# Attention and a gated MLP on one core: which loads release which weight parts in the first tile

## The chip, the cores and the metric

The kernel runs on 1 core of one Trainium2 chip. The metric is the time of one execution on the device in microseconds (us); the time of a kernel is the median of its runs.

## The reference

Sliding-window causal attention (window 64) over 8 batches of 8 heads, 576 tokens and 64 values per head, and then a feed-forward layer with a gate on its result:

```python
B, H, S, D = q.shape                                   # 8, 8, 576, 64
scores = np.matmul(q, k.transpose(0, 1, 3, 2)) / np.sqrt(D)
rel = pos[:, None] - pos[None, :]
scores = np.where((rel >= 0) & (rel < 64), scores, -1e9)
attn = np.exp(scores - scores.max(-1)); attn /= attn.sum(-1) + 1e-09
x = np.matmul(attn, v).transpose(0, 2, 1, 3).reshape(B * S, H * D)   # 4608 x 512
h = x @ w_in                                           # w_in: 512 x 2048
g = h * np.clip(h + 3.0, 0.0, 6.0) / 6.0
out = g @ w_out                                        # w_out: 2048 x 512
```

Inputs and output are f32; the matmuls of the kernel are in bf16.

## The kernel before

**Tiles.** The layer is computed in nine tiles T of 512 tokens, the attention in eight batches of 576. `s1(T)` (L523) makes the 16 column blocks `fc` of the gated hidden layer: four matmuls with `win16` per block, one activation on ScalarE and one gate operation on VectorE. Block `fc` uses columns 128 fc to 128 fc + 127 of w_in. `s2(T, order)` (L560) multiplies by `wout16`; a piece of it is four matmuls for one of four token groups and one quarter of w_out's rows. For tile 0 the order is BY_PART (L582): all four token groups with quarter 0, then all with quarter 1, and so on. Attention pieces of the next batches are put by hand between the pieces of `s1` and `s2`: T_ and TT (transposes of Q and K on TensorE, with their copies out of PSUM), S_ (scores), N_ (values and normalisation), X_ (transpose of the result into `xT`), R_ and RR (the transposes of the remainder rows, tokens 512 to 575 of each head, which are loaded apart).

**Order.** The schedule is manual: every engine executes its instructions in the order of the program text, and so do the DMA queues of SyncE (SP) and GpSimd (POOL). A queue whose next load waits holds all that stand behind it. `after(x, y, why)` (L68) makes instruction x wait until y is done; for a load, until it has landed.

**Weights.** They are loaded on POOL's queue, cast from f32 to bf16 on the way, in four parts each: w_in by 512 columns (`load_w_in`, L225), w_out by 512 rows (`load_w_out`, L231). A part has 1 MB in memory and 512 KB in SBUF. Part i of w_in serves blocks 4 i to 4 i + 3. POOL also casts all Q, K and V to bf16, so in its order casts (which wait for loads) and weight loads alternate: w_in part 0 at L645, part 1 at L648, parts 2 and 3 at L650, w_out part 0 at L721, parts 1 to 3 at L723.

**Q, K, V.** They are loaded on SP's queue. Batch 0 comes first (L140, L82). For batch 1 `load_qk_for_pe(1, 4)` (L100) returns in this order: `ins[0]`, `ins[1]`: Q and K of heads 0 to 3 (512 KB each, L107); `ins[2]`, `ins[3]`: remainder rows of Q and K (128 KB each, L113); `ins[4]`, `ins[5]`: Q and K of heads 4 to 7. Then follow `insr[:2]`, the remainder rows of Q and K of batch 0 (L151), and `insv`: the remainder of V of batch 0, and V of batch 1 (L94, L82). Behind them stand the loads of batches 2 and up (L94), and the DMA transposes and output writes.

**The releases.** `ins[0]` and `ins[1]` wait for w_in part 1 (L704); `ins[2:]` and `insr[:2]` for w_out part 0 (L724); `insv` for w_out part 2 (L726). Since SP goes in order, each wait holds all later loads too.

**The stretch of the change (L697 to L765).** `m = s1(0, ...)` makes tile 0. Its first groups of matmuls and the blocks 0 to 3 are 6 steps of the generator, of which 2 are taken at once (L698, L700); `run(m, 12)` (L731) goes to the end of block 11. Then `TT(bt, 0)` transposes Q and K of the first pair of heads of batch 1, which needs the POOL casts of heads 0 to 3; two blocks follow, `TT(bt, 1)`, and the last two blocks. Then `s2(0)` starts: scores of two pairs, four pieces with w_out part 0, `RR(bt)` (L760) with the remainder rows of batch 1 (cast at L728), and the pieces with part 1.

Of the kernel before, what the change touches and what calls it, by code (L numbers as in the profile page):

```python
# [24 lines left out]
def kernel(  # L25
# [14 lines left out]
    NG = H // 2  # L40
# [27 lines left out]
    def after(ins, dep, why):  # L68

        tc.add_manual_dep(  # L70
            ins.ins, dep.ins.name,
            mybir.DependencyInfo(mybir.DependencyClass.Sync, mybir.DependencyReason.DATA),
            reason=why,
        )
# [25 lines left out]
    def load_qk_for_pe(b, heads):  # L100
        qst = stage.tile([P, H, R * D], F32, name="qst", tag="qst")
        kst = stage.tile([P, H, R * D], F32, name="kst", tag="kst")
        rst = stage.tile([P, H, D], F32, name="rst", tag="rst")
        ins = []
        for h0 in range(0, H, heads):
            for dst, src in ((qst, q), (kst, k)):
                ins.append(nc.sync.dma_start(  # L107
                    out=dst[:, h0 : h0 + heads, :],
                    in_=src[b, h0 : h0 + heads, 0:SM, :].rearrange("h (p j) d -> p h (j d)", j=R),
                ))  # L110
            if h0 == 0:
                for i, src in enumerate((q, k)):
                    ins.append(nc.sync.dma_start(  # L113
                        out=rst[i * SR : (i + 1) * SR, :, :],
                        in_=src[b, :, SM:S, :].rearrange("h s d -> s h d"),
                    ))
        return (qst, kst, rst), ins

    def load_v_by_head(b):
        vst = stage.tile([P, KB, H, D], F32, name="vst", tag="vst")  # L120
        ins = load_blocks(vst, v, b, (KB - 1,), SR) + load_v(b, vst, 0, H)
        return vst, ins
# [23 lines left out]
    def load_rest_of_first():  # L146
        rst = stage.tile([P, H, D], F32, name="rst0", tag="rst0")
        rvst = stage.tile([P, H, D], F32, name="rvst", tag="rvst")
        ins = []
        for dst, p0, src in ((rst, 0, q), (rst, SR, k), (rvst, SR, v)):  # L150
            ins.append(nc.sync.dma_start(  # L151
                out=dst[p0 : p0 + SR, :, :], in_=src[0, :, SM:S, :].rearrange("h s d -> s h d"),
            ))
        return rst, rvst, ins
# [70 lines left out]
    def load_w_in(f0, f1, g0, g1):  # L225
        return nc.gpsimd.dma_start(
            out=win16[:, g0:g1, f0:f1],
            in_=moe_w_in[g0 * P : g1 * P, f0:f1].rearrange("(g p) f -> p g f", p=P),
        )

    def load_w_out(c0, c1):  # L231
        return nc.gpsimd.dma_start(
            out=wout16[:, c0:c1, :],
            in_=moe_w_out[c0 * P : c1 * P, :].rearrange("(c p) j -> p c j", p=P),
        )


    vcopy, pcopy, acopy = nc.vector.tensor_copy, nc.gpsimd.tensor_copy, nc.scalar.copy
# [284 lines left out]
    def s1(T, first=()):  # L523
        t0 = T * TB
        gT = gpool.tile([P, NFC, TB], BF16, name="gT")
        gTs[T] = gT

        def mms(fc, hT, gs):
            for g in gs:
                nc.tensor.matmul(  # L530
                    hT, lhsT=win16[:, g, fc * P : (fc + 1) * P],
                    rhs=xT[:, g, t0 : t0 + TB], start=(g == 0), stop=(g == NG - 1),
                )

        def gate(out, hT, shape):
            t1 = (t1pool, t2pool)[len(shape) - 2].tile(shape, BF16, name=f"t{len(shape) - 1}")
            nc.scalar.activation(out=t1[:], in_=hT, func=RELU, bias=half[:], scale=1.0 / 6.0)  # L537
            nc.vector.scalar_tensor_tensor(  # L538
                out=out, in0=t1[:], scalar=1.0, in1=hT, op0=MIN, op1=MULT,
            )  # L540

        if first:
            sts = [ps_st.tile([P, 2, 512], F32, name=f"st{u}") for u in range(2)]
            for gs in first:
                for fc in range(4):
                    mms(fc, sts[fc // 2][:, fc % 2, :], gs)
                yield
            for u in range(2):
                for fc in (2 * u, 2 * u + 1):
                    mms(fc, sts[u][:, fc % 2, :], (NG - 1,))  # L550
                gate(gT[:, 2 * u : 2 * u + 2, :], sts[u][:], [P, 2, TB])
                yield
                yield
        for fc in range(4 if first else 0, NFC):
            hT = s1_bank(fc, T)
            mms(fc, hT, range(NG))
            gate(gT[:, fc, :], hT, [P, TB])
            yield

    def s2(T, order):  # L560

        gT, accs = gTs[T], {}
        for ts, f0, f1 in order:
            if f0 == 0:
                accs[ts] = h_bank()[:] if T == 0 and ts > 1 else next(oa)
            for fc in range(f0, f1):
                nc.tensor.matmul(  # L567
                    accs[ts], lhsT=gT[:, fc, ts * P : (ts + 1) * P], rhs=wout16[:, fc, :],
                    start=(fc == 0), stop=(fc == NFC - 1),
                )  # L570
            if f1 == NFC:
                osb = osbp.tile([P, DM], F32, name="osb")
                acopy(out=osb[:], in_=accs[ts])  # L573
                u0 = T * TB + ts * P
                if T:
                    nc.sync.dma_start(out=out[u0 : u0 + P, :], in_=osb[:])
                else:
                    held.append((u0, osb))
            yield
# [4 lines left out]
    def run(gen, n=10 ** 6):  # L584
        for _ in range(n):
            if next(gen, "end") == "end":
                break
# [32 lines left out]
    def TT(bt, g, banks=None):  # L620
        T_(bt, g, banks)
        do(bt, "q", g)
        do(bt, "k", g)
# [12 lines left out]
    def cast_pairs(bt, st, h0, heads):  # L636
        bt.cast_qk(st, 0, h0, heads, pcopy)
        bt.cast_qk(st, 1, h0, heads, pcopy)


    bt, st = Batch(0), stage0
# [3 lines left out]
    w_in = [load_w_in(0, 512, 0, NG)]  # L645
# [1 line left out]
    bt.cast_v(vst0, 4, 6, pcopy)  # L647
    w_in.append(load_w_in(512, 1024, 0, NG))  # L648
    bt.cast_v(vst0, 6, 8, pcopy)
    w_in += [load_w_in(512 * i, 512 * (i + 1), 0, NG) for i in (2, 3)]  # L650
    pcopy(out=bt.V[0:SR, KB - 1, :, 0:D], in_=bt.V[SR:P, KB - 2, :, 0:D])

    def S0_(g, u):
# [43 lines left out]
    m = s1(0, ((0, 1), (2,)))  # L697
# [5 lines left out]
    st1, ins = load_qk_for_pe(1, 4)  # L703
# [3 lines left out]
    rst0, rvst0, insr = load_rest_of_first()  # L707
    vst1, insv = load_v_by_head(1)
    insv = insr[2:] + insv
# [5 lines left out]
    for h in range(2):  # L715
        nc.vector.tensor_copy(
            out=mask[:, (KB - 1) * (h + 1) - 1, P:QW], in_=mask1[:, WINDOW : 2 * WINDOW],
        )
    bt, st = Batch(1), st1
    bt.cast_qk(st, 0, 0, 4, pcopy)  # L720
    w_out = [load_w_out(0, 4)]  # L721
    bt.cast_qk(st, 1, 0, 4, pcopy)
    w_out += [load_w_out(4 * i, 4 * i + 4) for i in (1, 2, 3)]  # L723
    for x in ins[2:] + insr[:2]:  # L724
        after(x, w_out[0], "the weights go first")
    for x in insv:  # L726
        after(x, w_out[2], "the weights go first")
    bt.cast_rest(st, pcopy)  # L728
    cast_pairs(bt, st, 4, 4)
    bt0.cast_rest((None, None, rst0), pcopy)  # L730
    run(m, 12)  # L731
    TT(bt, 0, oa_tr)
    run(m, 2)
    TT(bt, 1, oa_tr)
# [21 lines left out]
    m = s2(0, BY_PART)  # L756
# [124 lines left out]
```

## Time and profile before

| | us |
|---|---|
| median of 7 runs | 326.93 |
| lowest, highest | 323.26, 328.76 |
| profiled execution, whole | 328.82 |
| its span, first to last instruction | 327.1 |
| TensorE (PE) busy | 307.1 |
| VectorE (DVE), ScalarE (ACT), GpSimd (POOL) busy | 178.9, 177.7, 90.0 |

| load on POOL's queue | issued at | landed after |
|---|---|---|
| w_in part 0 | 11.0 | 6.5 |
| w_in part 1 | 13.4 | 7.8 |
| w_in part 2 | 14.7 | 9.1 |
| w_in part 3 | 15.5 | 12.4 |
| w_out part 0 | 29.8 | 5.4 |
| w_out part 1 | 31.5 | 8.4 |
| w_out part 2 | 32.3 | 10.9 |
| w_out part 3 | 33.0 | 13.5 |

| load on SP's queue | issued at | landed after |
|---|---|---|
| Q, K of heads 0 to 3, batch 1 | 21.3, 21.8 | 7.3, 8.3 |
| remainder rows of Q, K, batch 1 | 35.2, 36.0 | 8.5, 10.7 |
| Q, K of heads 4 to 7, batch 1 | 36.7, 37.5 | 11.5, 13.0 |
| remainder rows of Q, K, batch 0 | 40.0, 43.1 | 11.1, 8.7 |
| V of batch 1, 8 loads | 48.1 to 53.7 | 3.6 to 3.7 |

All times within the trace count from the start of the span. PE is the matmul side of TensorE, PEld its weight loads, POOLq and SPq the two queues that issue DMAs. A name such as `st` or `h` is a PSUM tile, `win` and `wout` are the weights in SBUF, `qst`, `kst`, `vst` and `rst` the loaded f32 inputs, `qn`, `kn` and `rn` their casts. In "out<-in" the first is written. The granted clock is TensorE's, as a share of full speed.

### The profile page before, as it was taken

The page shows a single profiled execution, that of the slowest core. Times are in us where ns is not written, and L with a number is a line of the kernel's source. Part 1 is how long each engine was busy: PE and PEld are TensorE (multiplying, and loading weights), DVE is VectorE, ACT ScalarE, POOL GpSimd, SP SyncE. Part 2 cuts the span into 40 slices and gives each one's busy share as a digit, 9 for nine tenths or more (in the row PEclk, how much of TensorE's full clock was granted, in tenths as well). Part 3 has the DMA queues.
Part 4 walks back from the last instruction along what each step waited for, and adds up shares of the span by engine and source line. Part 5 has one row for each costly group of instructions (what it writes and reads, how often), then busy time and mean ns, then how long its engine had stood idle before and what let it go on. Part 6 is the DMA issues. An engine that isn't in the chain of part 4 may idle for free.

```text
span 327.1 us, 5618 instructions
## 1 busy us (share of the span) xinstructions
PE 307.1 (94%) x2162; PEld 149.7 (46%) x2162; DVE 178.9 (55%) x334; ACT 177.7 (54%) x264; POOL 90.0 (28%) x128
## 2 busy tenths in 40 slices
PE   7996929979999999999999999999999999999995
PEld 3543414554455445544444454445444544444442
DVE  4666404556674585657835773687178618505800
ACT  3765504537773685379416951794279327516711
POOL 6804117464047143405600353044300000000000
PEclk9999878979999999999999999999999999999999
DMA  7994999899899999889749998999950260020011
GB/s 252 206 195 140 178 255 195 190 214 235 177 196 211 243 213 219 210 173 206 144 125 257 199 212 164 248 198 203 193 132 2 72 118 22 0 93 37 0 66 64
DMA packets 151515, 52.80 MB, mean 161 GB/s; under 512 B 138944, under 2 KB 147136, under 8 KB 151488
## 3 DMA queue, kind: packets, MB, share of 16 engines
q1 hardware_dynamic: 146672, 46.94, 71.2%
q0 software_dynamic: 4544, 5.24, 9.2%
q8 instruction: 17, 0.28, 0.4%
q10 hardware_dynamic: 272, 0.26, 0.2%
q14 instruction: 10, 0.08, 0.1%
HBM read 36.70 MB, written 9.44 MB: 141 GB/s over the span
## 4 chain that ended last, share of the span: by engine, by line
PE 76%; DMA 12%; DVE 6%; ACT 2%; SPq 1%; issue 1%; POOL 1%; POOLq 0%
PE acc L567 17%; PE o L567 16%; PE h L530 15%; PE st L530 6%; PE o L530 6%; PE acc L530 6%; PE st L353 4%; DMA qst<-in_q_dram 4%; DMA rst<-in_k_dram 3%; DMA win<-in_moe_w_in_dram 2%; PE h L383 2%; DMA wout<-in_moe_w_out_dram 2%; DVE gT L538 2%; DVE pT L371 2%; DVE opg L405 2%; PE h L388 1%
## 5 line engine op out<-in xcount | busy, mean ns | idle before, releaser
L530 PEld LDWEIGHTS <-win 128*128 128x128 bf16 x576 | 55.9, 99 | 67.9 <-issue 4.2
L567 PEld LDWEIGHTS <-gT 128*128 128x128 bf16 x576 | 52.9, 98 | 57.9 <-issue 1.6
L567 PE MATMUL o<-wout,gT 128*128 128x512 bf16 x272 | 66.8, 383 | 0.0
L567 PE MATMUL acc<-wout,gT 128*128 128x512 bf16 x272 | 64.8, 383 | 0.0
L530 PE MATMUL h<-xT,win 128*128 128x512 bf16 x264 | 63.1, 379 | 0.0
L361 ACT ACTIVATE pT<-st 128x768 bf16<-128x768 f32 x64 | 48.7, 808 | 15.5 <-PE st L353 15.4
L538 DVE SCALAR_TENSOR_TENSOR gT<-t,st 128x512 bf16<-128x512 bf16 (+1 forms) x26 | 20.7, 809 | 62.2 <-ACT t L537 62.2
L537 ACT ACTIVATE t<-h,half 128x512 bf16<-128x512 f32 x66 | 44.7, 691 | 8.4 <-PE h L530 7.9
L538 DVE SCALAR_TENSOR_TENSOR gT<-t,h 128x512 bf16<-128x512 bf16 x66 | 44.6, 685 | 7.9 <-ACT t L537 7.9
L371 DVE TENSOR_TENSOR pT<-pT,mask 128x1536 bf16<-128x1536 bf16 x28 | 33.2, 1184 | 22.6 <-ACT pT L361 22.5
L257 POOL CAST qn<-qst 128x512 bf16<-128x512 f32 x24 | 15.6, 689 | 78.5 <-DMA qst<-in_q_dram 78.5
L530 PE MATMUL st<-xT,win 128*128 128x512 bf16 x128 | 32.6, 399 | 0.4 <-DVE gT L538 0.3
L573 ACT COPY osb<-acc 128x512 f32<-128x512 f32 x17 | 10.0, 586 | 41.8 <-PE acc L567 41.8
L573 ACT COPY osb<-o 128x512 f32<-128x512 f32 x17 | 10.0, 588 | 30.2 <-PE o L567 30.2
L405 DVE TENSOR_TENSOR opg<-h,rec 128x320 bf16<-128x320 f32 x48 | 23.6, 491 | 1.7
L537 ACT ACTIVATE t<-st,half 128x512 bf16<-128x512 f32 (+1 forms) x26 | 20.1, 785 | 7.8 <-PE st L530 7.8
L530 PE MATMUL o<-xT,win 128*128 128x512 bf16 x92 | 23.6, 379 | 0.3 <-DVE gT L538 0.3
L530 PE MATMUL acc<-xT,win 128*128 128x512 bf16 x92 | 23.6, 379 | 0.0
L383 PEld LDWEIGHTS <-pT 128*128 128x128 bf16 x256 | 17.7, 98 | 8.8 <-DVE opg L405 1.9
L257 POOL CAST kn<-kst 128x512 bf16<-128x512 f32 x24 | 16.1, 708 | 17.6 <-DMA kst<-in_k_dram 17.6
L247 POOL CAST V<-vst 128x512 bf16<-128x512 f32 (+1 forms) x14 | 16.4, 1170 | 14.3 <-DMA vst<-in_v_dram 12.4
L353 PE MATMUL st<-QT,KT 64*128 64x192 bf16 (+2 forms) x312 | 17.6, 232 | 1.0 <-ACT KT L321 0.5
(100 smaller groups left out, 281.5 us busy)
## 6 DMA issues: line engine op xcount, KB each, us to landing
out_dram<-osb SPq DMA_DIRECT2D x32, 256.0 KB, 2.3
qst<-in_q_dram SPq DMA_DIRECT2D x28, 256.0 KB, 4.6
kst<-in_k_dram SPq DMA_DIRECT2D x27, 256.0 KB, 5.3
vst<-in_v_dram SPq DMA_DIRECT2D x24, 256.0 KB, 5.4
vst<-in_v_dram SPq DMA_DIRECT2D x23, 128.0 KB, 3.7
win<-in_moe_w_in_dram POOLq DMA_DIRECT2D x4, 512.0 KB, 8.5
wout<-in_moe_w_out_dram POOLq DMA_DIRECT2D x4, 512.0 KB, 9.7
qst<-in_q_dram SPq DMA_DIRECT2D x2, 512.0 KB, 9.4
```

Of the source, the lines that this page charges most:

```text
L247: copy(out=self.V[:, 0 : KB - 1, h0:h1, 0:D], in_=vst[:, 0 : KB - 1, h0:h1, :])
L257: pcopy(out=n[:, g, 0 : KB - 1, :, :].rearrange("p k h d -> p k (h d)"), in_=s[:, 0 : KB - 1, 2 * g : 2 * g + 2, :].rearrange("p k h d -> ...
L353: nc.tensor.matmul(st[:, h, o0 : o0 + n], lhsT=bt.KT[h * D : (h + 1) * D, g, k0 : k0 + P], rhs=bt.QT[h * D : (h + 1) * D, g, q0 : q0 + n], ...
L361: nc.scalar.activation(out=pT[:, :, 2 * u : 2 * u + 2, 0:QW], in_=st[:, :, 0:w].rearrange("p h (k w) -> p h k w", k=2), func=EXP, scale=scale,
L371: nc.vector.tensor_tensor(out=pT[:, :, :, 0:QW], in0=pT[:, :, :, 0:QW], in1=mask[:].rearrange("p (h k) w -> p h k w", h=2), op=MULT,)
L383: nc.tensor.matmul(ob, lhsT=pT[:, h, qb, 0:P], rhs=V[:, qb, 2 * g + h, :], start=True, stop=(qb == 0),)
L405: nc.vector.tensor_tensor(out=opgs[bt.b, g][:, 0:nb, h, :], in0=ov[:, :, 0:D], in1=rec[:, 0:nb].unsqueeze(2).to_broadcast([P, nb, D]), op= ...
L530: nc.tensor.matmul(hT, lhsT=win16[:, g, fc * P : (fc + 1) * P], rhs=xT[:, g, t0 : t0 + TB], start=(g == 0), stop=(g == NG - 1),)
L537: nc.scalar.activation(out=t1[:], in_=hT, func=RELU, bias=half[:], scale=1.0 / 6.0)
L538: nc.vector.scalar_tensor_tensor(out=out, in0=t1[:], scalar=1.0, in1=hT, op0=MIN, op1=MULT,)
L567: nc.tensor.matmul(accs[ts], lhsT=gT[:, fc, ts * P : (ts + 1) * P], rhs=wout16[:, fc, :], start=(fc == 0), stop=(fc == NFC - 1),)
L573: acopy(out=osb[:], in_=accs[ts])
```

## The change

The last part of w_in and the last three of w_out are released by loads of Q and K, and these by other weight parts than before:

- w_in part 3 is issued on POOL later: after the loads of batch 1 are set up, ahead of the first cast of batch 1, and it waits for `ins[0]` (Q of heads 0 to 3).
- `ins[2:]` wait for w_in part 3 instead of w_out part 0.
- The cast of the remainder rows (`cast_rest`) moves ahead of w_out parts 1 and 2 on POOL; these wait for `ins[4]` (Q of heads 4 to 7).
- w_out part 3 moves behind the casts of Q and K of heads 4 to 7.
- `insr[:2]` wait, as `insv` do, for w_out part 2.
- `run(m, 11)` instead of 12: block 11 follows `TT(bt, 0)`, block 13 follows `TT(bt, 1)`.

```diff
     bt.cast_v(vst0, 6, 8, pcopy)
-    w_in += [load_w_in(512 * i, 512 * (i + 1), 0, NG) for i in (2, 3)]
+    w_in.append(load_w_in(1024, 1536, 0, NG))
     pcopy(out=bt.V[0:SR, KB - 1, :, 0:D], in_=bt.V[SR:P, KB - 2, :, 0:D])
...
     bt, st = Batch(1), st1
+    w_in.append(load_w_in(1536, 2048, 0, NG))
+    after(w_in[3], ins[0], "the first heads go first")
     bt.cast_qk(st, 0, 0, 4, pcopy)
     w_out = [load_w_out(0, 4)]
     bt.cast_qk(st, 1, 0, 4, pcopy)
-    w_out += [load_w_out(4 * i, 4 * i + 4) for i in (1, 2, 3)]
-    for x in ins[2:] + insr[:2]:
-        after(x, w_out[0], "the weights go first")
-    for x in insv:
+    bt.cast_rest(st, pcopy)
+    for x in ins[2:]:
+        after(x, w_in[3], "the weights go first")
+    w_out += [load_w_out(4 * i, 4 * i + 4) for i in (1, 2)]
+    after(w_out[1], ins[4], "the last heads go first")
+    for x in insr[:2] + insv:
         after(x, w_out[2], "the weights go first")
-    bt.cast_rest(st, pcopy)
     cast_pairs(bt, st, 4, 4)
+    w_out.append(load_w_out(12, 16))
     bt0.cast_rest((None, None, rst0), pcopy)
-    run(m, 12)
+    run(m, 11)
     TT(bt, 0, oa_tr)
     run(m, 2)
     TT(bt, 1, oa_tr)
```

## The prediction

> **What bounds the kernel now.** I read, in this order, the page's slices, the waits of TensorE, the chain of work in the first 72 us, the busy table by microsecond, and the landing times of the loads. The waits (engine and line that waited, releaser: us in total, times, longest):
>
> ```profile
> PE st L298 <- POOL rn L293: 6.0, 1, 6.0
> PE st L463 <- DVE opg L405: 2.0, 1, 2.0
> PE o L316 <- POOL qn L286: 1.5, 1, 1.5
> PE acc L316 <- POOL kn L286: 1.3, 1, 1.3
> ```
>
> TensorE is busy for 307.1 of 327.1 us; all its waits of over 1.3 us lie before 71 us. The stage table (us, then busy us of PE, PEld, DVE, ACT, POOL, the granted clock, DMA share, GB/s) shows the one hole, and a later stage without any:
>
> ```profile
> 41.50:47.50 6.00, 0.00 (x0) 0.00 (x0) 0.00 (x0) 0.00 (x0) 0.62 (x1) 0.80 1.16 271
> 171.00:203.00 32.00, 32.00 (x235) 15.70 (x233) 19.78 (x36) 18.50 (x28) 10.71 (x13) 1.00 1.04 207
> ```
>
> So what moves the restart at 47.5 us moves the end, unless a later load catches up. The chain (start, us, what) tells what the hole waits for:
>
> ```profile
> 13.42 7.85 DMA win<-in_moe_w_in_dram
> 21.32 7.35 DMA qst<-in_q_dram
> 28.82 0.98 POOL qn L286
> 29.80 5.38 DMA wout<-in_moe_w_out_dram
> 35.98 10.74 DMA rst<-in_k_dram
> 46.84 0.62 POOL rn L293
> 47.51 0.61 PE st L298 x4
> ```
>
> It is DMA all along: Q of heads 0 to 3, then w_out part 0, then the remainder rows of K, which take 10.7 us for 128 KB beside the three other parts of w_out. Between the links the DMA stands nearly still (last two columns):
>
> ```profile
> 26.00:27.00 1.00, 1.00 (x7) 0.45 (x5) 1.00 (x3) 0.82 (x2) 0.00 (x0) 1.00 0.99 327
> 28.00:29.00 1.00, 0.40 (x2) 0.00 (x0) 0.81 (x2) 0.82 (x2) 0.18 (x1) 1.00 0.10 36
> 30.00:31.00 1.00, 0.31 (x4) 0.14 (x4) 0.65 (x1) 0.00 (x0) 1.00 (x2) 1.00 0.00 0
> 31.00:32.00 1.00, 0.35 (x4) 0.35 (x5) 0.04 (x1) 0.00 (x0) 1.00 (x2) 0.71 0.27 39
> 46.00:47.00 1.00, 0.00 (x0) 0.00 (x0) 0.00 (x0) 0.00 (x0) 0.16 (x1) 0.50 1.09 351
> ```
>
> About 3.5 us of DMA time (27.5 to 31) are unused.
>
> **Landing times of before,** issue plus time to landing from the views of the tiles: w_in parts 17.5, 21.3, 23.8, 27.9; Q and K of heads 0 to 3 28.7 and 30.1; w_out parts 35.2, 39.9, 43.2, 46.5; remainder rows of batch 1 43.7 and 46.7; Q and K of heads 4 to 7 48.2 and 50.5; remainder Q of batch 0 51.1.
>
> **The change, part by part.** No matmul, cast or load is added or removed; loads change places and releases.
>
> *w_in part 3 behind Q of heads 0 to 3.* Q was issued at 21.3 and landed 0.8 us after w_in part 3. Now w_in part 2 (23.8) is the last weight ahead: 24.6 by that row. From the other side: Q's 512 KB run for 1.5 us at the 350 GB/s of the table, after a 3.7 us landing of a 256 KB K load: 26.5. I take 25.3, nearer the row of the same load. On POOL the wait stands ahead of the Q cast, which needs the same Q, so only the issue (0.75) is put before it: issue 25.3, Q cast 26.1 to 27.1, w_out part 0 issued 27.1 to 27.9, K cast to 28.9.
>
> *w_in part 3 lands* 5.4 us after its issue (w_out part 0, alone on the wires, took 5.4; w_in part 0 beside V took 6.5): 30.7. w_out part 0 follows in the same queue; parts follow each other by 3.3 us (39.9, 43.2, 46.5): 34.0, or 32.5 if alone.
>
> *SP queue.* The remainder loads of batch 1 wait for w_in part 3 instead of w_out part 0: 30.7 instead of 35.2, and behind them at the spacings of before Q of heads 4 to 7 at 32.2 and its K at 33.0. One weight part is in flight beside them, not three. Q lands after w_out part 0 (34.0), the 256 KB of remainder rows (1.3 us at 200 GB/s) and its own 1.5 us: 36.8. Bounds: 3.7 us after issue (35.9), and the 11.5 us it took before (43.7). I lean to the low one, since that row had three parts of w_out beside it.
>
> *w_out parts 1 and 2* now wait on POOL for that Q. Behind the waiting instruction stand the casts of Q and K of heads 4 to 7 and w_out part 3. Issue 36.8, landing 5.4 later: 42.2 (8.4, the row of part 1, at worst: 45.2). Part 2 lands at 45.5. The casts run at 38.3 to 40.4; part 3 is issued at 40.4 and lands at 48.8.
>
> *TensorE.* Column block 11 of tile 0 moves behind the first transposes (0.86 us of matmuls beside a cast wait); block 12 waits for w_in part 3 (30.7). From block 12 to the hole TensorE took 32.05 to 41.5, 9.4 us, so the first four quarter sums are done by 40.1, or 1.4 us sooner if the eight matmuls of 3.27 us run at full clock. The remainder rows are cast by then. The 6.0 us wait is gone; late next is w_out part 1: the first matmuls that need it ran at 47.91 and now run at 42.2. **Gain 5.7 us.** Everything before it is covered by the wait for w_out part 1; were that gone, the gain would end at 40.1, 7.8 us.
>
> *Clock.* The matmuls after the hole ran at 0.50 until about 49.9: 1.91 us for four instead of 1.04. The new idle time is about 2 to 3 us, not 6. Between no half clock (1.1 us won) and a stretch like 32 to 34 (1.4 us lost), I count no difference. The Trainium skill (TensorE: Matmul & The Clock Gate, Part 1) has the half clock come after at least one idle window of about 3.4 us; by it alone the new wait would often stay at full clock and the gain be 6.8.
>
> *The queue that is moved past.* Remainder rows of batch 0, V of batch 1 and with them all later loads wait on SP for w_out part 2: 45.5 instead of 40.0. They were held before by K of heads 4 to 7 (50.5). The remainder Q of batch 0 lands 3.7 us (nearest V row) to 8.5 us (remainder row beside weights) after issue, 49.2 to 54.0, against 51.1: d = -1.9 to +2.9; with one part of w_out left to pass I take 0. Slack in before: first V pair cast by 55.9, used at 62.60, 6.7 us; K transposes of batch 2 landed 79.7, used 88.3; of batch 3 111.1, used 118.5, 7.4 us; of batch 4 136.6, used 149.2. So the gain is the smaller of 5.7 and 6.7 - d: it holds up to d = 1.0, and 3.8 is left at d = 2.9.
>
> *A rule that speaks otherwise.* The rows price a 512 KB weight load alone at 5.4 us. The Trainium skill (DMA: Bandwidth & Descriptors, Anatomy of one DMA) gives about 2.0 us plus bytes over 436 GB/s, an estimate of 3.2 us here. By it the two loads in the chain would land 4.4 us sooner, and no wait for w_out part 1 would be left. It also means that each hand-over costs about 2 us of latency, which speaks against releasing loads by landings.
>
> **Sum.** The profiled execution took 328.82 us, 327.1 of it span and 1.7 around it. 328.82 - 5.7 = 323.1. It stands 1.9 above the median of 326.93. As TensorE is full after 71 us, I place the spread of 323.26 to 328.76 in the start (an estimate); a median run may have 1.9 us less of this stall, a gain of 3.8 to 5.7. The middle, 4.75, off the median: 322.2 us.
>
> **Rivals.**
> 1. *No new wait:* w_out part 1 lands by 40.1. For it: Q and part 1 each at their lower bound give 35.9 + 5.4 = 41.3, so it needs still earlier links; against it: w_out part 0 is ahead. Gain 7 to 7.8: about 319.5.
> 2. *Given back:* V of batch 1 and what follows come late because their release moved from 40.0 to 45.5. For it: SP issues in order and slices up to 230 us show the DMA nearly full. Against it: Q of heads 4 to 7 is done 11 us sooner (48.2 to 36.8). At d = +5.5 the gain is 6.7 - 5.5 = 1.2: 325.7. The same time comes if Q of heads 0 to 3 lands no earlier than 28.7: the chain of 16.9 us (25.3 to 42.2) ends at 45.6, gain 2.3, 324.6.
> 3. *Slower:* Q of heads 4 to 7 is held on the wires by w_out part 0 and keeps its 11.5 us. It lands at 43.7, w_out part 1 at 49.1 to 52.1, TensorE restarts 1.2 to 4.2 after 47.91: 328.1 to 331.1. It decides from a Q landing later than 42.5. For it: 128 KB took 10.7 us beside weights; against it: one part, done by 34.
> 4. *The release does nothing:* excluded for w_in part 3, which had no wait and was issued at 15.5.
>
> **How the numbers follow.** A measurement of this kernel can tell about 1%, 3.3 us. Forecast 0.58 (0.06 of it within 1%, from the small end of its gain); rival 1 0.08, faster; rival 2 0.20 (0.18 within, 0.02 faster); rival 3 0.14 (0.10 slower, 0.04 within). Faster 0.62, same 0.28, slower 0.10. The range: low 318.5 (rival 1 and a microsecond of clock), high 327.5, past rival 2; the upper part of rival 3 is left out. The forecast's own: 320 to 324 (gain 3.8 less, or 5.7 plus, a microsecond of clock).
>
> **What would show it.** Right: the 6.0 us wait for rn is gone; Q of heads 0 to 3 lands near 25, w_in part 3 near 31, Q of heads 4 to 7 near 37; TensorE waits about 2 to 3 us for w_out at about 42; T = 1 starts (71.0 before) near 65.3; no load wait above 1 us after that. Wrong: w_out part 1 after 45, a wait for V or for the transposes of batch 2 or 3, or Q of heads 0 to 3 still at 28.

## The result, and the profile after

The changed kernel takes 323.86 us (median of 26 runs, 320.5 to 325.82), the kernel before 326.56 us (61 runs): ratio 0.9921, 95% interval 0.9900 to 0.9942. It is faster by 0.8%, 2.7 us, where 1.4% was forecast; 323.86 us lies just inside the 320 to 324 us that the prediction gave as the forecast's own. The profiled execution took 324.55 us, 322.8 of it span, against 328.82 and 327.1.

The waits of TensorE after the change (engine and line, releaser: us in total, times, longest):

```profile
PE o L567 <- DMA wout<-in_moe_w_out_dram: 5.8, 1, 5.8
PE st L463 <- DVE opg L405: 2.0, 1, 2.0
PE o L168 <- DVE xT L163: 1.3, 1, 1.3
```

The 6.0 us wait for the remainder rows and the two waits for casts (1.5 and 1.3) are gone. One of 5.8 us for w_out part 1 has taken their place. The chain (start, us, what) shows how it comes about:

```profile
24.51 5.27 DMA win<-in_moe_w_in_dram
29.80 0.71 SPq L113
31.23 6.81 DMA qst<-in_q_dram
38.33 5.50 DMA wout<-in_moe_w_out_dram
43.87 1.86 PE o L567 x4
```

Q of heads 0 to 3 lands at 24.2, more than four microseconds sooner than before, and w_in part 3 is issued on it at 24.5. From there each load of the chain is released by the landing of the last: w_in part 3 lands at 29.8, Q of heads 4 to 7 at 38.0, w_out part 1 at 43.8. In the stage table (us, busy us of PE, PEld, DVE, ACT, POOL, granted clock, DMA share, GB/s) two of the three hand-overs are holes in the DMA, and after the wait TensorE runs at half clock:

```profile
25.00:26.00 1.00, 1.00 (x7) 0.42 (x5) 1.00 (x3) 0.81 (x2) 0.96 (x2) 1.00 0.17 25
36.00:38.00 2.00, 2.00 (x13) 1.04 (x12) 0.00 (x0) 0.03 (x1) 0.61 (x1) 1.00 0.65 205
38.00:40.00 2.00, 0.12 (x3) 0.01 (x1) 0.29 (x1) 0.37 (x1) 1.67 (x3) 1.00 0.03 11
40.00:42.00 2.00, 0.00 (x0) 0.00 (x0) 0.00 (x0) 0.00 (x0) 2.00 (x3) 1.00 0.98 162
44.00:46.00 2.00, 2.00 (x10) 0.58 (x8) 0.00 (x0) 0.00 (x0) 0.00 (x0) 0.50 1.21 196
48.00:50.00 2.00, 2.00 (x11) 0.79 (x12) 0.70 (x2) 0.81 (x1) 0.00 (x0) 0.52 1.13 219
```

Between the landing of Q and the first bytes of w_out part 1 the DMA moves 11 GB/s for two microseconds; after the landing of Q of heads 0 to 3 it moves 25 GB/s for one. At the hand-over of 29.8 there is no hole, since w_out part 0 is under way.

### The profile page after: what moved, and what is told of

It is laid out like the page before. It is cut to its first block, busy times and chain, and to the rows that moved or that the text cites. A ratio compares the mean times of both kernels' runs of the same rounds, so it can differ in the third digit from the quotient of the medians.

```text
span 322.8 us, 5617 instructions
## 1 busy us (share of the span) xinstructions
PE 306.5 (95%) x2162; PEld 149.3 (46%) x2162; DVE 176.3 (55%) x334; ACT 177.7 (55%) x264; POOL 89.2 (28%) x128
## 4 chain that ended last, share of the span: by engine, by line
PE 79%; DMA 8%; DVE 4%; issue 3%; ACT 2%; SPq 2%; POOL 1%; POOLq 0%
PE acc L567 18%; PE o L567 17%; PE h L530 15%; PE st L530 6%; PE o L530 6%; PE acc L530 6%; PE st L353 4%; DMA qst<-in_q_dram 4%; PE h L383 2%; DMA wout<-in_moe_w_out_dram 2%; DVE gT L538 2%; DMA win<-in_moe_w_in_dram 2%; PE h L567 1%; PE h L388 1%; DVE opg L405 1%
## 5 line engine op out<-in xcount | busy, mean ns | idle before, releaser
L361 ACT ACTIVATE pT<-st 128x768 bf16<-128x768 f32 x64 | 48.8, 809 | 21.6 <-PE st L353 21.5
L371 DVE TENSOR_TENSOR pT<-pT,mask 128x1536 bf16<-128x1536 bf16 x28 | 30.5, 1088 | 27.4 <-ACT pT L361 27.4
L257 POOL CAST qn<-qst 128x512 bf16<-128x512 f32 x24 | 16.3, 716 | 76.0 <-DMA qst<-in_q_dram 72.3
L530 PE MATMUL st<-xT,win 128*128 128x512 bf16 x128 | 32.2, 393 | 0.9 <-DMA win<-in_moe_w_in_dram 0.5
L573 ACT COPY osb<-acc 128x512 f32<-128x512 f32 x17 | 10.0, 587 | 40.9 <-PE acc L567 40.9
L573 ACT COPY osb<-o 128x512 f32<-128x512 f32 x17 | 10.0, 588 | 30.2 <-PE o L567 30.2
L537 ACT ACTIVATE t<-st,half 128x512 bf16<-128x512 f32 (+1 forms) x26 | 20.1, 785 | 6.9 <-PE st L530 6.6
L247 POOL CAST V<-vst 128x512 bf16<-128x512 f32 (+1 forms) x14 | 17.8, 1270 | 15.7 <-DMA vst<-in_v_dram 8.2
```

Of the source, the lines that this page charges most:

```text
L247: copy(out=self.V[:, 0 : KB - 1, h0:h1, 0:D], in_=vst[:, 0 : KB - 1, h0:h1, :])
L257: pcopy(out=n[:, g, 0 : KB - 1, :, :].rearrange("p k h d -> p k (h d)"), in_=s[:, 0 : KB - 1, 2 * g : 2 * g + 2, :].rearrange("p k h d -> ...
L361: nc.scalar.activation(out=pT[:, :, 2 * u : 2 * u + 2, 0:QW], in_=st[:, :, 0:w].rearrange("p h (k w) -> p h k w", k=2), func=EXP, scale=scale,
L371: nc.vector.tensor_tensor(out=pT[:, :, :, 0:QW], in0=pT[:, :, :, 0:QW], in1=mask[:].rearrange("p (h k) w -> p h k w", h=2), op=MULT,)
L530: nc.tensor.matmul(hT, lhsT=win16[:, g, fc * P : (fc + 1) * P], rhs=xT[:, g, t0 : t0 + TB], start=(g == 0), stop=(g == NG - 1),)
```

## The experiments

Ratios are to the kernel before, with their 95% intervals.

**The w_in part alone.** Kernel before, with:

```diff
-    w_in += [load_w_in(512 * i, 512 * (i + 1), 0, NG) for i in (2, 3)]
+    w_in.append(load_w_in(1024, 1536, 0, NG))
...
     bt, st = Batch(1), st1
+    w_in.append(load_w_in(1536, 2048, 0, NG))
+    after(w_in[3], ins[0], "the first heads go first")
...
-    run(m, 12)
+    run(m, 11)
```

> Only the first part of the change: w_in part 3 waits for Q of heads 0 to 3 and block 11 moves behind the first transposes; all other releases as before. Theory (the chain of landings sets the restart, and the w_out parts are what slows the remainder rows): Q lands near 24.5, w_out part 0 near 33 instead of 35.2, then the remainder rows again take about 10.7 us beside three parts of w_out, so the wait for the cast of these rows stays and TensorE restarts near 44.5 to 45.5 instead of 47.5: 2 to 3 us faster than before, ratio 0.991 to 0.994, about all that the whole change gives. Rival (the gain comes from the second part, the remainder rows no longer beside three parts of w_out): restart not before 46.5, within 0.3% of before.

Measured 324.96 us, ratio 0.9926 (0.9884 to 0.9968). Its longest wait and the restart, from a profiled execution of 326.55 us:

```profile
PE st L298 <- POOL rn L293: 6.3, 1, 6.3
```

```profile
45.17 0.61 PE L298 MATMUL st<-ident,rn 128*128 128x128 bf16 x4 [6.25 <-POOL rn L293]
45.57 1.91 PE L567 MATMUL o<-wout,gT 128*128 128x512 bf16 x4
```

As expected, the old wait stays, the restart comes 2.3 us sooner, and alone this part gives about what the whole change gives. The way there is not the expected one: w_out part 0 landed at 34.8, not near 33, and the remainder rows were issued only 0.4 us sooner than before. What came sooner are w_out parts 1 to 3 (issued from 28.95 instead of 31.5, the last landed at 43.8 instead of 46.5), and the rows beside them landed at 44.4 instead of 46.7. That does not yet say that the other part gives nothing.

**All but the w_in part.** Changed kernel, with parts 2 and 3 of w_in again together at 15, and `run(m, 12)`:

```diff
-    w_in.append(load_w_in(1024, 1536, 0, NG))
+    w_in += [load_w_in(512 * i, 512 * (i + 1), 0, NG) for i in (2, 3)]
...
-    w_in.append(load_w_in(1536, 2048, 0, NG))
-    after(w_in[3], ins[0], "the first heads go first")
...
-    run(m, 11)
+    run(m, 12)
```

> All of the change but its first part: w_in part 3 is issued at 15.5 again and block 11 stays where it was; the remainder rows and Q of heads 4 to 7 wait for w_in part 3, w_out part 1 for that Q. Theory (each release by a landing leaves the DMA idle for about 1.5 to 3 us, so one hand-over less is better): w_in part 3 lands near 27.9, Q of heads 0 to 3 near 28.7, the remainder rows start at 28 and Q of heads 4 to 7 lands near 36 to 37, w_out part 1 near 42 to 43: restart near 42.5, 1 us or more sooner than in the whole change, ratio to before 0.985 to 0.991. Rival (the first part is what makes room for the rest): restart at 45.5 or later, ratio 0.994 or above.

Measured 318.80 us, ratio 0.9772 (0.9723 to 0.9821): better than the theory, and the best so far. The issue of the remainder rows on SP, of w_out part 0 and of parts 1 and 2 on POOL, and the first matmuls with part 1:

```profile
26.39 0.71 SPq L113 DMA_DIRECT2D rst<-in_q_dram  x1
```

```profile
28.50 0.74 POOL L232 DMA_DIRECT2D wout<-in_moe_w_out_dram  x1
32.48 1.48 POOL L232 DMA_DIRECT2D wout<-in_moe_w_out_dram  x2 [0.94 <-DMA qst<-in_q_dram]
```

```profile
40.75 1.03 PE L567 MATMUL o<-wout,gT 128*128 128x512 bf16 x4
```

w_in part 3, issued early, has landed by 26.4, so the rows start 3.4 us sooner than in the change and *ahead* of w_out part 0. No weight part is under way when they start: rows land at most 4.0 us after issue (6.3 in the change), Q of heads 4 to 7 at 32.2 (38.0). It is w_out part 0, issued 0.7 us behind Q, that takes longer, 8.5 us. Part 1 is there when TensorE asks; the longest wait for w_out is 1.3 us, for part 0. The two parts of the change work against each other. Block 11 changes its place with the w_in part in this run and the one before; its place was not tried by itself.

**w_out part 1 without its wait.** Changed kernel, with:

```diff
+    w_out.append(load_w_out(4, 8))
     bt.cast_rest(st, pcopy)
...
-    w_out += [load_w_out(4 * i, 4 * i + 4) for i in (1, 2)]
-    after(w_out[1], ins[4], "the last heads go first")
+    w_out.append(load_w_out(8, 12))
+    after(w_out[2], ins[4], "the last heads go first")
```

> The whole change, but w_out part 1 waits for nothing and stands ahead of the cast of the remainder rows; part 2 takes its wait for Q of heads 4 to 7. Theory (the wait for w_out part 1 is the price of the hand-over: landing of Q, issue, first bytes): part 1 lands near 36.5 behind part 0, the remainder rows near 38 to 39, Q of heads 4 to 7 near 40; the 5.8 us wait falls to about 1 to 2 us for the cast of the remainder rows, TensorE restarts near 39.5 and the kernel is 3 to 5 us faster than with the whole change, ratio to before 0.977 to 0.984. Rival (given back later: the loads of V and of batches 2 and 3 are no earlier, so TensorE waits for them instead): restart near 39.5 but new waits for V or for the transposes of batch 2 or 3, ratio 0.988 to 0.994. Second rival (the remainder rows are slowed by two parts of w_out as before): restart after 43, no gain.

Measured 319.76 us, ratio 0.9818 (0.9768 to 0.9868). Three of its waits:

```profile
PE st L298 <- POOL rn L293: 1.2, 1, 1.2
PE st L383 <- POOL V L247: 0.9, 1, 0.9
PE st L353 <- DMA KT<-kn: 0.8, 1, 0.8
```

The wait for part 1 was the price of its hand-over: with the rows 2 us later than in the change TensorE still goes on with part 1 at 39.97. The rival holds in part: for the first time TensorE waits for V of batch 1 and for the K transposes of batch 2, 0.9 and 0.8 us. So giving back begins where TensorE is about 8 us ahead of the kernel before.

**Dummy matmuls in the wait.** Changed kernel, with 24 matmuls that nobody reads behind `RR(bt, st_tr(0))`:

```diff
     RR(bt, st_tr(0))
+    dummy = ps_st.tile([P, 2, 512], F32, name="st1")
+    for _ in range(24):
+        nc.tensor.matmul(dummy[:, 0, :], lhsT=xT[:, 0, 0:P], rhs=xT[:, 0, 0:TB], start=True, stop=True)
     run(m, 1)
```

> The whole change, with 24 matmuls added whose results nobody reads, put on TensorE into the wait for w_out part 1 (24 times 0.216 us is 5.2 us at full clock, the wait is 5.75 us). Theory (part of the gain was lost to the half clock after the wait, 43.87 to about 48.5): the granted clock stays at 1.00 from 36 to 55, the stretch from the restart to the transposes of heads 4 to 7 takes about 5.0 us instead of 7.0, and the kernel is 1.5 to 2 us faster than the whole change, ratio to before 0.985 to 0.988. Rival (what is lost lies in the landings, and a faster stretch runs into the next load, w_out part 2 or 3): no change against the whole change, or a wait for w_out of 1 to 2 us at part 2.

Measured 322.42 us, ratio 0.9881 (0.9834 to 0.9928); the interval overlaps that of the change, so the size is not settled by the times. In the trace the half clock behind the wait is gone:

```profile
44.88 1.03 PE L567 MATMUL o<-wout,gT 128*128 128x512 bf16 x4
49.98 1.03 PE L567 MATMUL o<-wout,gT 128*128 128x512 bf16 x4
```

```profile
44.00:46.00 2.00, 2.00 (x15) 0.86 (x13) 0.00 (x0) 0.00 (x0) 0.00 (x0) 1.00 1.13 186
```

From the first matmul with part 1 to the first with part 2 it takes 5.1 us at full clock, 7.9 in the change (43.87 to 51.75), 7.0 before (47.91 to 54.89). The restart is 1.0 us later than in the change, since in this run Q of heads 0 to 3 landed later (w_in part 3 was issued at 25.9 instead of 24.5), so the two traces differ in more than the clock.

**One release alone.** Kernel before, with one line changed:

```diff
     for x in ins[2:] + insr[:2]:
-        after(x, w_out[0], "the weights go first")
+        after(x, w_in[3], "the weights go first")
```

> The kernel before with one release changed: the remainder rows of batch 1, Q and K of heads 4 to 7 and the remainder rows of batch 0 wait for w_in part 3 instead of w_out part 0; w_in part 3 is issued at 15.5 and the w_out parts stand and wait as before. Theory A (what pays is that these loads start at 26.4 instead of 35.2, in the gap ahead of w_out part 0; holding w_out parts 1 and 2 back is not needed): remainder rows land near 31, Q of heads 4 to 7 near 32 to 34, w_out part 0 near 37, part 1 near 40.5; no wait for the cast of the rows, restart without a wait of over 1.5 us, ratio to before 0.972 to 0.980, as in the run without the w_in part (0.977). Theory B (the hold of the w_out parts is what pays): the rows are slowed beside w_out, restart after 44, ratio above 0.988.

Measured 319.21 us, ratio 0.9809 (0.9755 to 0.9862); theory A, at its edge, but with a wait of 2.9 us where none above 1.5 was expected. The issue of the rows on SP, and that wait:

```profile
26.21 0.71 SPq L113 DMA_DIRECT2D rst<-in_q_dram  x1
```

```profile
PE o L567 <- DMA wout<-in_moe_w_out_dram: 2.9, 1, 2.9
```

All w_out parts are issued by 32.3 without a hold, and the rows are still not slowed (4.0 us at most): they were first. The wait is for w_out part 0, which landed 9.5 us after its issue.

**The hold alone.** Kernel before, with w_out parts 1 and 2 held for `ins[4]`, part 3 behind the casts and `insr[:2]` behind part 2, as in the change; `ins[2:]` wait for w_out part 0 as before.

```diff
-    w_out += [load_w_out(4 * i, 4 * i + 4) for i in (1, 2, 3)]
-    for x in ins[2:] + insr[:2]:
+    bt.cast_rest(st, pcopy)
+    for x in ins[2:]:
         after(x, w_out[0], "the weights go first")
-    for x in insv:
+    w_out += [load_w_out(4 * i, 4 * i + 4) for i in (1, 2)]
+    after(w_out[1], ins[4], "the last heads go first")
+    for x in insr[:2] + insv:
```

> The kernel before with the hold alone: w_out parts 1 and 2 wait for Q of heads 4 to 7, part 3 stands behind the casts of heads 4 to 7, the remainder rows of batch 0 wait with V for w_out part 2; but the remainder rows of batch 1 and Q and K of heads 4 to 7 still wait for w_out part 0, and w_in part 3 is issued at 15.5. Theory A (the early start of the rows is what pays): rows start at 35 and land near 38, Q of heads 4 to 7 near 40, w_out part 1 is issued there and lands near 45.5 to 46: TensorE restarts near 46, 1 to 2 us sooner than before, ratio 0.992 to 0.998. Theory B (the hold pays): ratio below 0.985.

Measured 326.77 us, ratio 1.0022 (0.9984 to 1.0061). The rows land fast (4.2 us at most), but the wait only changes its name:

```profile
PE o L567 <- DMA wout<-in_moe_w_out_dram: 5.6, 1, 5.6
```

TensorE restarts at 46.87, 1.0 us sooner than before, and then takes 7.7 us to the first matmul with part 2, where it took 7.0 before. The hold gives nothing by itself. Theory B falls; A's estimate of 0.992 to 0.998 was somewhat too good.

**Rows that wait for nothing.** Changed kernel, with:

```diff
-    for x in ins[2:]:
-        after(x, w_in[3], "the weights go first")
```

> The whole change, but the remainder rows of batch 1 and Q and K of heads 4 to 7 wait for nothing: they follow K of heads 0 to 3 on SP at 22. Theory (in the change the rows wait from 22 to 29.8 for w_in part 3, which itself waits for the landing of Q, and that double hand-over is what the w_in part costs): rows and Q of heads 4 to 7 land by 29 to 31, w_in part 3 near 31 to 33, w_out part 0 near 35 to 36, part 1, no longer held, near 38 to 40; the 5.8 us wait for w_out part 1 falls below 2 us, and the ratio to before is 0.972 to 0.982. Rival (Q of heads 0 to 3 and w_in part 3 are delayed by as much): waits for the Q cast or w_in part 3 of over 3 us, ratio 0.986 or above.

Measured 322.12 us, ratio 0.9892 (0.9836 to 0.9949). The rival, for w_in part 3 (Q of heads 0 to 3 is not delayed):

```profile
PE st L530 <- DMA win<-in_moe_w_in_dram: 4.7, 1, 4.7
```

```profile
25.13 0.74 POOL L226 DMA_DIRECT2D win<-in_moe_w_in_dram  x1 [8.71 <-DMA qst<-in_q_dram]
30.65 1.48 POOL L232 DMA_DIRECT2D wout<-in_moe_w_out_dram  x2 [0.86 <-DMA qst<-in_q_dram]
```

Q of heads 4 to 7 lands at 30.6, but w_in part 3, issued at 25.1 while SP's loads are under way, takes 9.5 us to land instead of 5.3. The wait changes its name again. The time is no worse than with the release (0.9921, the intervals overlap), so the release is not needed here; taking it away only does not help.

**The best version, with dummies in the short wait.** The second experiment's kernel, with 8 matmuls that nobody reads ahead of `rest_x(bt0)`:

```diff
     X_(bt, 0, 1)
+    dummy = ps_h.tile([P, 512], F32, name="h0")
+    for _ in range(8):
+        nc.tensor.matmul(dummy[:], lhsT=xT[:, 0, 0:P], rhs=xT[:, 0, 0:TB], start=True, stop=True)
     rest_x(bt0)
```

> The run without the w_in part (0.977 to before), with 8 matmuls added whose results nobody reads, ahead of the last transpose of batch 0's remainder rows, where TensorE waits 2.1 us for VectorE; at full clock they take 1.7 us. Theory (the short wait there brings a half-clock window of 3.4 us over the first matmuls of tile 1, which took 3.43 us for 8 instead of 1.89): granted clock 1.00 in that stretch, 1.0 to 1.6 us faster, ratio to before 0.971 to 0.975. Rival (the 8 matmuls delay the transposes behind them by as much as the clock gives): ratio 0.977 or above.

Measured 317.69 us, ratio 0.9775 (0.9719 to 0.9830): no difference from 0.9772 that the measurement can tell. The trace shows the clock as expected: the first group of tile 1 takes 1.89 us, against 3.43 without the dummies. Two other runs had 1.89 us without dummies, though (last section), so one trace does not show that they did it.

```profile
62.81 0.29 PE L463 MATMUL st<-ident,opr 64*128 64x64 bf16 x4 [0.18 <-DVE opg L405]
64.09 1.89 PE L530 MATMUL st<-xT,win 128*128 128x512 bf16 x8
```

```profile
61.34 3.43 PE L530 MATMUL st<-xT,win 128*128 128x512 bf16 x8
```

The last line is from the run without dummies. Its profile has a wait of 1.3 us for w_out part 0, the one with dummies 2.5 us for w_out and 1.4 for w_in, so the landings of these two executions differ by more than the 1.5 us of clock.

## Why the prediction was right in sign and too large

The direction and the mechanism stand: the wait for the rows goes, w_out part 1 is late next, and no load wait appears after 71 us. The gain was set at 4.75 us off the median and measured 2.7. None of the rivals came: w_out part 1 was waited for, Q of heads 4 to 7 did not keep its 11.5 us, and nothing was given back. By the prediction's own steps:

- *Q of heads 0 to 3* at 25.3: it landed at 24.2. It took 4.0 us from its issue, as 25.3 less 21.3 had it, but it was issued at 20.2, since w_in part 1 landed 1.1 us sooner in this trace. That landing lies between 20.1 and 21.5 us over the ten traces, with w_in part 3 behind it in the queue or not, so the 1.1 us were luck. *w_in part 3* at 30.7: 29.8. *w_out part 0* at 34.0: 34.2. These were right.
- *SP queue, Q of heads 4 to 7* at 36.8: **this step failed.** It was issued at 31.2, a microsecond sooner than predicted, and landed at 38.0: 6.8 us, where the working allowed 4.6. It had been put nearer its low bound because only one weight part was beside it. One part is enough to cost. In the runs in which a weight part releases the rows, this Q took 4.4 to 5.3 us with no weight part under way at its issue (four runs), 6.0 and 6.8 with one (dummies in the wait, the change), 8.4 with two (w_out part 1 without its wait), 9.5 and 11.5 with three (the w_in part alone, before). The working also counts the bytes of the rows and of Q, 0.79 MB, but none of K of heads 4 to 7, issued 0.7 us behind: from 34 to 38 us the DMA moved about 1.0 MB (296 and 205 GB/s). How the 2.2 us divide between the two is not shown.
- *w_out part 1* at 42.2: issued 38.3 (36.8 predicted), landing 5.5 us later as predicted (5.4), at 43.8. The gain at the restart is 47.91 - 43.87 = 4.0 us instead of 5.7.
- *Clock,* counted as no difference: the wait was 5.75 us, not 2 to 3, since TensorE ran at full clock until 38.1 and came earlier to the same hole. The stretch behind it took 7.9 us instead of 7.0: 0.9 us lost, and 3.1 left. It was within the stated bounds (1.1 won to 1.4 lost), on the wrong side. The prediction had also read the half clock of before as ending at about 49.9; the row of 50 to 52 us puts its end near 51.9:

```profile
50.00:52.00 2.00, 2.00 (x12) 0.49 (x8) 0.85 (x1) 0.81 (x1) 1.19 (x2) 0.52 0.93 160
```

So about 4.0 us behind the restart ran at half clock before (47.91 to 51.9) and 6.0 after (43.87 to 49.9); the 2.0 us more cost about 1.0. The Trainium skill (TensorE: Matmul & The Clock Gate, Part 1) has half clock follow an idle window of about 3.4 us; for this wait of 5.75 us the trace agrees, with half clock from about 43.1 until about 49.9.
- *The queue that is moved past:* d was taken as 0; the remainder Q of batch 0 landed at 50.4 (51.1 before), and the loads of batch 2 are transposed from 72.07 on, against 71.86 before. (The first of the eight V loads of before took 5.3 us, not 3.6 to 3.7 as the table of before says; only the low bound of d was worked out from that row.) TensorE comes 3.1 us sooner to them and does not wait for them: the slack was there, as worked out.
- *From profile to median.* The two profiled spans differ by 4.3 us, more than 3.1. The rest lies in stages that the change does not touch: before, TensorE waited 1.1 us for VectorE between 130 and 175 us, after not at all (last section). The copies of the results out of PSUM (L573) run 3.1 us ahead of before up to 135 us (131.85 against 134.93), and 4.4 from 165 us on (161.04 against 165.40). The prediction put the 1.9 us by which its profile stood above the median wholly into the start; about 1.2 us of the profile lay here.
- *The rule on the cost of a DMA,* an estimate of 3.2 us for such a part from the Trainium skill (DMA: Bandwidth & Descriptors, Anatomy of one DMA): w_in part 3 and w_out part 1, each issued with no other weight part under way, took 5.3 and 5.5 us. The measured row was the right price.

What the prediction did not see is that the parts oppose each other. It priced the w_in part as a gain by Q's landing, correctly, and did not ask what the rows would do if w_in part 3 had stayed early: they would have started at 26.4, in the DMA gap that the table showed at 28 to 31, ahead of w_out part 0. The one-line experiment gives 1.9% by that alone. With the rows released by w_in part 3 in all four, the early issue of w_in part 3 gives 0.9772 with the hold of w_out part 1 and 0.9809 without it; the late issue gives 0.9921 with the hold and 0.9818 without it (third experiment, where parts 2 and 3 stay held). So it is the late issue and the hold of part 1 together that lose: each alone costs nothing that these runs can tell. Whether a hand-over's two idle microseconds could be shortened was not tried.

## What to carry to other kernels

A load that is released by a landing pays its own issue, first bytes and landing after that landing, here 5.3 to 5.5 us per 512 KB weight part, with the DMA nearly idle for part of it; so release by something that has landed anyway, and let the loads that the next step needs go ahead of the bulk ones instead of beside them. When a change has several parts, price each against the kernel without the others: here one part took away what the other needed. A wait of TensorE can cost more than its length: in all four traces with an empty wait of 5.6 to 6.3 us in the first tile, half clock followed it.

## What the runs showed of the hardware

**A short wait can bring half clock too.** After a wait of 2.0 us between small matmuls (65.55, changed kernel) the first eight matmuls of tile 1 took 3.44 us, where they take 1.89 at full clock:

```profile
65.55 0.29 PE L463 MATMUL st<-ident,opr 64*128 64x64 bf16 x4 [1.97 <-DVE opg L405]
66.83 3.44 PE L530 MATMUL st<-xT,win 128*128 128x512 bf16 x8
```

It need not: of the eight traces with this wait of 2.0 us, six show the half clock, two (one release alone, rows that wait for nothing) do not. What decides is not shown. The runs of the changed kernel differ with the clock: three had a mean granted clock of 0.995 and spans of 318.7 to 320.0 us, nineteen had 0.984 and 320.7 to 324.1. A mean of 0.984 over 322.8 us is about 10.3 us at half clock (an estimate); the trace has 6.8 from 43.1 on and 3.4 at tile 1. A mean of 0.995 leaves about 3.2 us, one stretch less. Part of the spread of this kernel thus goes with the number of half-clock stretches in a run; which of them the shorter runs lacked is not shown, since only one run has a trace.

**A load can stand behind those of the other queue.** A POOL load issued while SP's loads were under way landed after 9.5 us (w_in part 3, rows that wait for nothing) and 8.5 us (w_out part 0, second experiment), against 5.3 to 5.5 alone. In the first of the two all data packets from 25.2 to 30.0 us are of SP's queue, and the first of POOL's comes 5.2 us after the issue; in the change it comes after 1.4 and 1.7 us. Why it does not get its share sooner is not shown.

**VectorE and GpSimd.** A mask multiply of 0.96 us on VectorE took 2.66 us where GpSimd's wide cast of V had started just before it. In the kernel before, VectorE and then POOL:

```profile
131.12 2.66 DVE L371 TENSOR_TENSOR pT<-pT,mask 128x1536 bf16<-128x1536 bf16 x1 [0.71 <-ACT pT L361]
```

```profile
131.08 1.90 POOL L247 CAST V<-vst 128x2048 bf16<-128x2048 f32 x1 [3.81 <-DMA vst<-in_v_dram]
```

It happened again at 160.16 (2.62 us, cast from 160.07), and TensorE then waited 0.9 us. Both times the multiply ends 0.8 us after the cast. In the changed kernel the first pair misses each other (multiply from 128.05 to 129.01, cast from 129.97). In the second the multiply starts first, keeps its 0.96 us, and it is the cast that takes longer:

```profile
156.76 0.96 DVE L371 TENSOR_TENSOR pT<-pT,mask 128x1536 bf16<-128x1536 bf16 x1 [0.17 <-ACT pT L361]
```

```profile
156.90 2.58 POOL L247 CAST V<-vst 128x2048 bf16<-128x2048 f32 x1 [2.37 <-DMA vst<-in_v_dram]
```

The other traces agree: the multiply was held where the cast started first (the w_in part alone and the rows that wait for nothing, 2.5 and 2.6 us, with the same wait of TensorE again), and the cast where the multiply did (the hold alone and the last experiment, 2.37 and 2.14 us, without it). So of this pair the second to start was the one held up, in all seven meetings. That a shift of 3 us in the start decides which comes first was read from the traces, not tried by itself.
